# Attention and MoE on one core: a silu issued behind the next unit's copy in the first product, and the last batch's queries loaded later

## The chip, the cores and the metric

The kernel runs on one core of a Trainium2 chip. Times are device microseconds (us) of an execution. The five engines of the core that matter here are TensorE (PE, matmuls), VectorE (DVE), ScalarE (ACT), GpSimd (POOL) and SyncE (SP); POOL does no arithmetic here to speak of, it issues transfers, as SP does. All comparisons below are between runs in the fast state; one run fell into a slow state, with a lower granted clock of PE, and is named as such.

## The reference, cut to what matters

```python
# attention: batch 8, heads 8, seq 576, head_dim 64; keys and values pooled by 8
k_p = k.reshape(B, H, Sp, pool, D).mean(axis=3)
v_p = v.reshape(B, H, Sp, pool, D).mean(axis=3)
scores = scale * np.matmul(q, k_p.transpose(0, 1, 3, 2))
attn = softmax(scores)                          # cut
x = np.matmul(attn, v_p)                        # then (tokens 4608, 512)
# MoE: w_in 512 x 2048, w_out 2048 x 512
h = x @ w_in                                    # "first product"
g = h * (1.0 / (1.0 + np.exp(-h)))              # silu
out = g @ w_out                                 # "second product"
```

## The kernel before

Tokens are worked off in nine visits of 512 (t = 0 to 8). A visit has a first product (`up`), then a second one (`down_quarters`); the attention of the next batch is threaded through the second. Parts of both products are done by a scheme with seven products of quarters in place of eight. In the first product a "unit" does this for two column blocks at a time: its stages are named by digits, and `s` is a silu. `r_sb`, `rr_sb`, `t_sb` and `c_sb` are its intermediate sums, and `x_sum` are five sums of quarters of the tokens, made on DVE when a visit begins. `raw` holds keys or values before pooling, `kp` the pooled keys, `q_bf` a batch's queries and `qT` their transposes.

```python
def stage(y, n):
    if n == "2":
        product(y, 2, "P", True)                    # PE into PSUM bank P
        nc.scalar.copy(r_sb, ps["P"])               # ACT
    elif n == "5":
        product(y, 5, "Q", True)
        tt(out=rr_sb, in0=ps["Q"], in1=r_sb, op=ALU.add)      # DVE
    elif n == "1":
        product(y, 1, "R", True)
        tt(out=t_sb, in0=ps["R"], in1=rr_sb, op=ALU.subtract)
    ...
    elif n == "3":
        product(y, 3, "Q", False)                   # into Q again
        hidden(y, 0, 1, ps["Q"])                    # silu on ACT
    elif n == "7":
        product(y, 7, "P", False)
        tt(out=c_sb[0], in0=ps["P"], in1=t_sb, op=ALU.add)
        hidden(y, 0, 0, c_sb[0])                    # silu of the first sum
    elif n == "6":
        product(y, 6, "Q", False)
        tt(out=c_sb[1], in0=ps["Q"], in1=t_sb, op=ALU.add)
    else:
        hidden(y, 1, 1, c_sb[1])

# visits 2 to 8: plain blocks G, units 0 and 1
items = (G(12, 13) + [(0, "251")] + G(14) + [(0, "43")] + G(15) + [(0, "76")]
         + [(1, "2")] + [(0, "s")] + [(1, "51")] + G(0) + [(1, "43")] + G(1)
         + [(1, "76")] + G(2) + [(1, "s")] + G(3))
```

Each engine executes its own list in the order of the program. Other work (query transposes, loads, pooling) is put in as fillers at numbered steps of PE's work. The loads of the batch after next, in visits 1 to 5:

```python
def load_one(b, name):       # first half of the pooling window, plain load
    ...
    load_rows(nc.sync, raw, source(b, name)[:, :, :PH])
    ...
def load_rest(b, name):      # second half, added in flight to the first
    nc.gpsimd.dma_start(out=batches[b][f"{name}_raw"],
                        in_=source(b, name)[:, :, PH:], accum_op=ALU.add)
...
f_up.append((0, lambda: load_one(a + 1, "k")))
f_up.append((1, lambda: load_q(a + 1)))      # last batch: eight transfers of 32 x 18 x 64
f_up.append((2, lambda: load_rest(a + 1, "k")))
f_down.append((11, lambda: load_one(a + 1, "v")))
f_down.append((12, lambda: load_rest(a + 1, "v")))
...
for stage in range(2):
    f_down.append((100, lambda stage=stage: pool_k(a + 1, stage)))   # DVE reads raw
```

The stores of the output go out on SP too, sixteen a visit, ahead of the next `load_one` of k.

The softmax here doesn't subtract the row's maximum and nothing guards it: scores larger than these inputs give would overflow.

## Time and profile before

| | before |
|---|---|
| median of the first three runs | 288.31 us (288.19 to 288.97) |
| span of the profiled run | 287.0 us |
| PE busy | 279.4 us, 97% |
| length of visits 2, 3, 4, 5 | 29.4 us each |

PE is busy nearly throughout, so its busy share says little about what can be won. The useful reading is: find the steps between PE's instructions that are longer in one place than in another place with the same work. The prediction does this and shows its lines.

### The profile page before, as it was taken

How to read it: one execution, taken by the hardware profiler on the slowest of the kernel's cores; microseconds unless marked ns; L12 is line 12 of the kernel's file. 1: busy time of each engine (PE TensorE's matmuls, PEld its weight loads, DVE VectorE, ACT ScalarE, POOL GpSimd, SP SyncE). 2: the span in 40 equal slices, each digit the busy share in tenths (PEclk: the TensorE clock that was granted, in tenths of full speed). 3: DMA queues.
4: the chain of work that ended last, by engine and by line, in shares of the span. 5: the costliest groups of instructions: out<-in, count | busy, mean ns of one | idle time of the engine just before them, and what ended most of it. 6: DMA issues, size and time to landing. Idle time of an engine off the chain costs nothing.

```text
span 287.0 us, 6919 instructions
## 1 busy us (share of the span) xinstructions
PE 279.4 (97%) x2773; PEld 196.0 (68%) x2793; DVE 225.6 (79%) x403; ACT 183.4 (64%) x359; POOL 52.6 (18%) x68
## 2 busy tenths in 40 slices
PE   8989999999999999999999999999999999999995
PEld 2438544466777677767888886687667867786684
DVE  3987854979969896979797969886988786846773
ACT  1577676468656876688568857794679558325700
POOL 8754317501020011101020107212000000000000
PEclk9999999999999999999999999999999999999999
DMA  8999999893749566973979396968830032006004
GB/s 210 269 262 231 217 310 172 221 216 53 148 67 208 124 91 106 136 209 60 140 122 211 73 151 112 164 121 162 161 77 0 2 86 63 2 5 142 2 1 148
DMA packets 35296, 37.70 MB, mean 131 GB/s; under 512 B 9952, under 2 KB 27616, under 8 KB 35264
## 3 DMA queue, kind: packets, MB, share of 16 engines
q0 software_dynamic: 21760, 20.86, 43.1%
q1 hardware_dynamic: 12928, 15.48, 22.3%
q10 hardware_dynamic: 576, 0.92, 1.1%
q8 instruction: 22, 0.36, 0.6%
q14 instruction: 10, 0.08, 0.1%
HBM read 36.70 MB, written 9.44 MB: 161 GB/s over the span
## 4 chain that ended last, share of the span: by engine, by line
PE 91%; DVE 4%; ACT 2%; issue 1%; DVEq 0%
PE hp_ps L546 23%; PE o_psP L654 15%; PE o_psQ L654 15%; PE u_psQ L488 7%; PE u_psP L488 6%; PE o_psR L654 5%; PE sc_ps L351 4%; PE warm_ps L703 4%; PE o_ps L581 3%; PE nu_ps L395 3%; PE den_ps L369 2%; PE u_psR L488 2%; DVE rr_sb L508 1%; ACT r_sb L505 1%; DVE w_sum L632 1%
## 5 line engine op out<-in xcount | busy, mean ns | idle before, releaser
L546 PE MATMUL hp_ps<-xT,w_in_sb 128*128 128x512 bf16 (+3 forms) x397 | 80.8, 338 | 1.4 <-ACT h_T L552 0.4
L552 ACT ACTIVATE h_T<-hp_ps 128x512 bf16<-128x512 f32 (+2 forms) x95 | 51.3, 545 | 27.2 <-PE hp_ps L546 26.3
L654 PEld LDWEIGHTS <-h_sum 128*128 128x128 bf16 x640 | 60.6, 98 | 11.9 <-issue 1.3
L546 PEld LDWEIGHTS <-w_in_sb 128*128 128x128 bf16 x412 | 39.3, 98 | 24.9 <-issue 1.4
L614 DVE TENSOR_TENSOR h_sum<-h_T 128x1024 bf16<-128x1024 bf16 (+1 forms) x72 | 50.8, 743 | 7.0 <-ACT h_T L552 7.0
L359 ACT ACTIVATE es<-sc_ps 72x384 bf16<-72x384 f32 (+1 forms) x100 | 39.0, 470 | 10.0 <-PE sc_ps L351 10.0
L488 PEld LDWEIGHTS <-w_sum 128*128 128x128 bf16 x300 | 29.3, 98 | 8.2 <-DVE x_sum L455 0.5
L654 PEld LDWEIGHTS <-h_T 128*128 128x128 bf16 x256 | 24.1, 98 | 4.4 <-issue 0.9
L496 ACT ACTIVATE h_T<-c_sb 128x512 bf16<-128x512 f32 x30 | 18.8, 628 | 11.6 <-DVE c_sb L520 11.6
L404 DVE TENSOR_TENSOR xT<-nu_ps,rec 128x384 bf16<-128x384 f32 (+1 forms) x50 | 24.0, 533 | 0.4
L378 ACT ACTIVATE lnd<-den_ps 128x384 f32<-128x384 f32 (+1 forms) x23 | 11.1, 484 | 20.2 <-PE den_ps L369 20.2
L153 DVE STREAM_TRANSPOSE qT<-q_bf 128x576 bf16<-128x576 bf16 x32 | 23.0, 754 | 0.0
L182 POOL DMA_DIRECT2D raw<-in_k_dram x5 | 7.0, 1405 | 66.3 <-DVE qT L153 31.2
L274 DVE TENSOR_TENSOR raw<-raw 128x384 f32<-128x384 f32 (+3 forms) x20 | 12.3, 616 | 7.2 <-DMA raw<-in_v_dram 3.6
L654 PE MATMUL o_psP<-w_out_sb,h_sum 128*128 128x256 bf16 x128 | 17.6, 273 | 0.0
L654 PE MATMUL o_psQ<-w_sum,h_sum 128*128 128x256 bf16 x128 | 16.7, 273 | 0.0
L654 PE MATMUL o_psQ<-w_out_sb,h_sum 128*128 128x256 bf16 x128 | 16.6, 273 | 0.0
L654 PE MATMUL o_psP<-w_sum,h_T 128*128 128x256 bf16 x128 | 16.5, 273 | 0.0
L654 PE MATMUL o_psQ<-w_sum,h_T 128*128 128x256 bf16 x128 | 16.5, 273 | 0.0
L182 POOL DMA_DIRECT2D raw<-in_v_dram x5 | 6.9, 1390 | 49.4 <-DMA raw<-in_v_dram 15.6
L654 PE MATMUL o_psR<-w_sum,h_sum 128*128 128x256 bf16 x128 | 15.7, 273 | 0.0
L558 POOL DMA_DIRECT2D out_dram<-o_sb x1 | 0.6, 628 | 81.8 <-issue 81.8
(77 smaller groups left out, 435.9 us busy)
## 6 DMA issues: line engine op xcount, KB each, us to landing
out_dram<-o_sb SPq DMA_DIRECT2D x128, 64.0 KB, 3.0
q_bf<-in_q_dram POOLq DMA_DIRECT2D x6, 576.0 KB, 11.1
raw<-in_k_dram SPq DMA_DIRECT2D x6, 512.0 KB, 5.7
raw<-in_k_dram POOLq DMA_DIRECT2D x5, 576.0 KB, 9.6
raw<-in_v_dram POOLq DMA_DIRECT2D x5, 576.0 KB, 9.1
raw<-in_v_dram SPq DMA_DIRECT2D x5, 512.0 KB, 8.2
w_in_sb<-in_moe_w_in_dram POOLq DMA_DIRECT2D x8, 256.0 KB, 8.3
w_out_sb<-in_moe_w_out_dram POOLq DMA_DIRECT2D x4, 512.0 KB, 13.8
```

Source lines behind the costliest of these rows:

```text
L153: nc.vector.transpose(out=st["qT"][:, a, f * QF : (f + 1) * QF].rearrange("r i c p -> r (i c p)"), in_=st["q_bf"][:, a, f * n : (f + 1) * n],)
L182: nc.gpsimd.dma_start(out=batches[b][f"{name}_raw"], in_=source(b, name)[:, :, PH:], accum_op=ALU.add,)
L274: nc.vector.tensor_add(out=raw[..., :w], in0=raw[..., :w], in1=raw[..., w : 2 * w])
L351: nc.tensor.matmul(sc[s][:, cs], lhsT=kz[b % 2][rows, g, c, :], rhs=st["qT"][rows, g, i0:i1, c, :], start=(c == 0), stop=(c == 1),)
L359: nc.scalar.activation(es[:, s, :], sc[s], func=AF.Exp, scale=score_scale)
L404: nc.vector.tensor_mul(out=xT[:, 2 * g0 + c : 2 * (g0 + ng - 1) + c + 1 : 2, cols], in0=nu[c][:, :w].rearrange("r (g n) -> r g n", g=ng), ...
L488: nc.tensor.matmul(ps[bank][:, u, :], lhsT=w[:, kk, 128 * u : 128 * (u + 1)], rhs=x[:, kk, :], start=first and u == 0 and kk == 0, stop=kk ...
L496: nc.scalar.activation(h_T[:, g : g + 2, j * NQ : (j + 1) * NQ], src, func=AF.Silu)
L546: nc.tensor.matmul(hp_ps[:, r0:r1], lhsT=w_in_sb[:, kk, g * 128 : (g + 1) * 128], rhs=xT[:, kk, x0 : x0 + r1 - r0], start=(kk == 0), stop= ...
L552: nc.scalar.activation(h_T[:, g, n0 : n0 + n], hp_ps[:, :n], func=AF.Silu)
L614: nc.vector.tensor_tensor(out=h_sum[n][:, ks, :], in0=quarter(*a, ks), in1=quarter(*b, ks), op=op)
L654: nc.tensor.matmul(ps[b][:, c, :], lhsT=left(n, kt, c), rhs=W_OUT[n][:, kt, :], start=b not in begun, stop=kt == k1 - 1, skip_group_check= ...
```

## The change

Its intent is twofold. Part A: in visits 2 to 8 the silu of unit 0's first sum is issued on ACT behind unit 1's copy `r_sb` instead of ahead of it (a new stage `h`). Part B: the query load of the last batch, the one made of eight small transfers, is issued at step 48 of visit 5's first product instead of step 1, and so behind the second half of k.

```diff
-                KF if len(it) == 3 else 2 * len(it[1].strip("s")) for it in items
+                KF if len(it) == 3 else 2 * len(it[1].strip("hs")) for it in items
...
                 tt(out=c_sb[0], in0=ps["P"], in1=t_sb, op=ALU.add)
-                hidden(y, 0, 0, c_sb[0])
...
+            elif n == "h":
+                hidden(y, 0, 0, c_sb[0])
...
-                    + [(0, "76")] + G(10) + [(0, "s")] + G(11, 0, 1, 2, 3)
+                    + [(0, "7h6")] + G(10) + [(0, "s")] + G(11, 0, 1, 2, 3)
...
-                    + [(1, "2")] + [(0, "s")] + [(1, "51")] + G(0) + [(1, "43")] + G(1)
-                    + [(1, "76")] + G(2) + [(1, "s")] + G(3)
+                    + [(1, "2")] + [(0, "hs")] + [(1, "51")] + G(0) + [(1, "43")] + G(1)
+                    + [(1, "7h6")] + G(2) + [(1, "s")] + G(3)
...
-                f_up.append((1, lambda: load_q(a + 1)))
+                f_up.append((48 if a + 1 == B - 1 else 1, lambda: load_q(a + 1)))
```

## The prediction

> **What bounds the kernel now.** I read the page's busy shares first, then the chain that ended last, then the timeline of the first product ("up") of visits 2 to 8. A visit is one pass of 512 tokens, nine in all (0 to 8).
>
> ```profile
> PE 279.4 (97%) x2773; PEld 196.0 (68%) x2793; DVE 225.6 (79%) x403; ACT 183.4 (64%) x359; POOL 52.6 (18%) x68
> ...
> PE 91%; DVE 4%; ACT 2%; issue 1%; DVEq 0%
> ```
>
> TensorE (PE) carries 91% of the chain. What a scheduling change can win is only the rest: stretches in which PE waits. The chain in order of time names one such stretch in every visit from 2 to 6: the copy r_sb on ACT (0.57), then rr_sb on DVE (0.70), then PE on u_psQ. Visit 3, by the timeline (start, length, engine, line, operation; weight loads and lines of no use here left out):
>
> ```profile
> 121.03 0.65 DVE L520 TENSOR_TENSOR c_sb<-u_psP,t_sb 128x512 f32<-128x512 f32 x1
> ...
> 121.61 0.67 DVE L524 TENSOR_TENSOR c_sb<-u_psQ,t_sb 128x512 f32<-128x512 f32 x1
> 121.72 0.63 ACT L496 ACTIVATE h_T<-c_sb 128x512 bf16<-128x512 f32 x1 [1.07 <-DVE c_sb L520]
> ...
> 122.26 0.57 ACT L505 COPY r_sb<-u_psP 128x512 f32<-128x512 f32 x1
> ...
> 122.86 0.69 DVE L508 TENSOR_TENSOR rr_sb<-u_psQ,r_sb 128x512 f32<-128x512 f32 x1 [0.57 <-ACT r_sb L505]
> 122.89 0.60 PE L488 MATMUL u_psP<-x_sum,w_in_sb 128*128 128x256 bf16 x4
> ...
> 123.60 0.60 PE L488 MATMUL u_psQ<-x_sum,w_in_sb 128*128 128x256 bf16 x4
> ```
>
> Read it from the bottom. The second unit's product 3 goes into the bank u_psQ. That bank must first be read by rr_sb, rr_sb needs r_sb, and the copy to r_sb stands on ACT behind the silu of the first unit's c_sb[0]. That silu waited 1.07 us for DVE, while u_psP (started 120.72, 0.60 long) was there to be copied from 121.32. Undisturbed, one product's start follows another's by 0.44; visit 7 shows it:
>
> ```profile
> 241.46 0.60 PE L488 MATMUL u_psP<-x_sum,w_in_sb 128*128 128x256 bf16 x4
> ...
> 241.90 0.60 PE L488 MATMUL u_psQ<-x_sum,w_in_sb 128*128 128x256 bf16 x4
> ```
>
> In visit 3 the step is 0.71, so PE loses 0.27. The same subtraction gives 0.27 in visit 2 (93.52 to 94.23), 0.22 in 4 (152.31 to 152.97), 0.27 in 5, 0.29 in 6 (211.66 to 212.39), and nothing in 7 and 8. There DVE has no query transposes ahead of c_sb, so it is on time. Sum 1.32 us.
>
> A second loss stands in visit 6 alone. It comes from the loads, so I read POOL's, SP's and DVE's timelines of visits 5 and 6:
>
> ```profile
> 174.31 1.37 POOL L182 DMA_DIRECT2D raw<-in_v_dram  x1 [11.37 <-DVE kp L193]
> 175.13 5.23 POOL L138 DMA_DIRECT2D q_bf<-in_q_dram  x7
> 185.68 0.67 POOL L138 DMA_DIRECT2D q_bf<-in_q_dram  x1 [5.32 <-DMA raw<-in_v_dram]
> 192.60 1.42 POOL L182 DMA_DIRECT2D raw<-in_k_dram  x1 [6.25 <-DVE vp L193]
> ...
> 184.94 1.24 SPq L173 DMA_DIRECT2D raw<-in_k_dram  x2
> ...
> 202.21 1.22 DVE L188 TENSOR_TENSOR raw<-raw 72x1024 f32<-72x1024 f32 x1 [0.56 <-DMA raw<-in_k_dram]
> ```
>
> The last batch's queries are eight small transfers instead of one. While they are in flight, the first half of k (issued 184.94) took 6.9 us to land against 5.7 for the same transfer in visit 4, and the accumulating second half was issued 7.7 us after it, against 6.4 in visit 4 (155.16 to 161.55). So DVE waited 0.56 at the pooling of k, its five x_sum came late, and PE paid. Against visit 2, counted from the start of the visit (84.71 and 202.22, the latter with the one matmul record that is missing put back), u_psR is 0.39 late, product 3 of unit 0 is 0.60 late, and unit 1 starts 0.60 late. That 0.60 is the whole loss.
>
> **What the Trainium skill says.** "PSUM — Partial Sum Buffer", section "Engine vs sequencer instructions": ScalarE and VectorE queues are strict FIFO. The trace agrees: u_psP was ready at 121.32 and ACT idle, yet the copy started at 122.26, after the silu ahead of it. "DMA: Bandwidth & Descriptors", section "Anatomy of one DMA — SWDGE (gpsimd) path": a DMA's semaphore wait happens on the issuing sequencer. Hence a waiting transfer holds up everything behind it on POOL; the 5.32 us before the eighth query transfer agrees. Same page, section "Queues, rings and completion order": the engines take turns among queues packet by packet and take one ring's descriptors in order. So queries behind an accumulating load in POOL's queue should land after it. The v half issued at 174.31 took 11.1 us to land (185.4), the first query transfer landed at about 186.0: agreed. The same page's "Specifications" puts the smallest transfer at line rate at 512 B; the last batch's query rows are 64 floats, 256 B. The trace agrees in part: this v half took 11.1 us with those queries behind it, against 9.2 and 9.1 in visits 3 and 4 with a single big query transfer behind it.
>
> **The change part by part.** No instruction is added or removed. The edit of the string strip only alters the number of steps counted, and no filler lies between the old and the new end. In visit 1 "7h6" puts the silu where it was. What moves is this.
>
> Part A, in visits 2 to 8: on ACT, r_sb's copy comes ahead of silu(c_sb[0]). Visit 2: ACT is free at 91.28, u_psP is done at 91.95, so the copy runs from about 92.0 to 92.57 instead of from 92.89 to 93.46. rr_sb then waits for c_sb[1] ahead of it on DVE, which starts at 92.24; such operations follow each other at 0.61, so rr_sb starts at 92.85 instead of 93.49, 0.64 earlier. The bank is free 0.74 after that start (93.49 to 94.23 in the old order), at 93.59. PE wants it at 93.52 + 0.44 = 93.96. The wait of 0.27 vanishes with 0.37 to spare. The silu of c_sb[0] moves from 92.35 to about 92.5, and that of c_sb[1] from 93.36 to about 93.0, so ACT ends this stretch earlier. The other visits have the same offsets. Gain: all of 0.27 + 0.27 + 0.22 + 0.27 + 0.29 = 1.32 us, nothing in 7 and 8. PE stays saturated behind the place, so I expect no give-back.
>
> Part B, in visit 5 alone: the second k half goes ahead of the queries on POOL. Its first half lands without query traffic. By visit 4's times (k issued 11.7 into the visit, 6.4 to the second half, 10.1 to landing) it lands 28.2 into the visit. DVE wants it 28.76 into visit 4 (143.44 to 172.20), and 28.5 once that visit is 0.27 shorter. So it arrives in time with 0.3 to spare, and 0.60 comes back, if visit 4's times hold. But seven query transfers are now issued right behind it, as they were behind the v half that needed 11.1 us. If that costs 1 to 2 us again, k is late by 0.7 to 1.7 and PE loses that much where it now loses 0.60. On top, POOL has eight semaphores that go round; by the waits in the changed program the eighth query transfer now waits for the k half to land, as it waited for the v half before. It lands about 6.5 after that (185.68, 6.5 to landing). With k landing near 200.6 of the new time that is 207.2. The second transpose of visit 6 needs it at about 206.9, or 207.3 before PE feels it through DVE's slack of 0.37. That is just on the edge. A late k delays the deadline too, so the two losses do not simply add.
>
> I weigh full recovery (+0.60) at a half, a small or equal loss (about 0) at three in ten, and a loss of some 0.7 beyond the present one at two in ten: 0.30 + 0 - 0.14, about 0.2 us.
>
> Sum: 1.32 + 0.2 = 1.5 us; 288.31 - 1.5 = 286.8.
>
> **The rivals.** First: both parts work in full. Then it is 1.32 + 0.60 = 1.9 us, 286.4. For it speaks that visit 4, without small queries, shows no wait at k. Second: the late queries become the new wait, k's second half slowed by the small packets behind it or the transposes of visit 6 waiting for the eighth transfer. For it speak the 11.1 us and the edge worked out above; the time would be 287.0 to 288.0, with visit 6 the longer one. Third: part A's wait is replaced by another, silu(c_sb[0]) now late for the h_sum operations or c_sb[1] on DVE holding rr_sb. Against it: h_sum starts at 94.89 in visit 2 and needs silus that end before 94, and rr_sb has 0.37 to spare. It would leave about half of the 1.32, so 287.5. Fourth: the gap is hidden anyway and the visit is as long as before. Against it: visits 2 to 5 are each 29.36 to 29.39 long, PE is on the chain through them, and no transfer is awaited there. It would be 288.3.
>
> **Range and chances.** The sure part gives 287.0, the full one 286.4. Repeats of the kernel before spread from 288.19 to 288.97. I take 286.0 to 287.9. A gain over 2% would need 5.8 us, three times the waits in reach; a loss over 2% would need queries late by several us. Faster 0.01, within 2% 0.98, slower 0.01.
>
> **What would show it.** Part A is right if in visits 2 to 6 the copy r_sb of unit 1 starts before the silu of c_sb[0], rr_sb follows c_sb[1] without waiting for ACT, the step from u_psP to u_psQ is 0.44, and visits 2 to 5 last about 29.1. Part B is right if DVE no longer waits for raw at the end of visit 5 and unit 1 of visit 6 starts 6.6 into it. It is wrong if that wait grows, or if a transpose of visit 6 shows a wait for q_bf's transfer. The prediction as a whole fails if the five steps close and the visits keep their length, or if visit 6 grows by more than the 1.3 that part A saves.

## The result, and the profile after

The changed kernel took 287.26 us in the median of six runs (286.08 to 287.70), the kernel before 288.55 (288.19 to 289.28) in six. The ratio is 0.9947, 95% interval 0.9922 to 0.9971. Ratios here and below are the mean time of one kernel's fast runs over that of the other's fast runs of the same rounds, so they are not quite the ratio of the medians quoted. Executions over 1.5% slower than the fastest of the same kernel are left out of the means. It is about 1.5 us faster: within 2%, and inside the predicted range.

In the changed kernel the sum `c_sb[1]` is at L523 instead of L524, and the lines behind the unit's stages are one higher (L546 became L547). Its page has these two lines (busy time, and the chain's shares by engine):

```profile
PE 278.0 (98%) x2773; PEld 196.0 (69%) x2793; DVE 225.1 (79%) x403; ACT 183.8 (65%) x359; POOL 52.2 (18%) x68
...
PE 94%; DVE 3%; ACT 1%; issue 1%; DVEq 0%
```

PE's share of the chain went from 91% to 94%; DVE's fell from 4% to 3% and ACT's from 2% to 1%. Visit 3 by the timeline, to be held against the same visit in the prediction:

```profile
120.42 0.65 DVE L520 TENSOR_TENSOR c_sb<-u_psP,t_sb 128x512 f32<-128x512 f32 x1
...
120.79 0.59 ACT L505 COPY r_sb<-u_psP 128x512 f32<-128x512 f32 x1 [0.77 <-PE u_psP L488]
...
121.00 0.67 DVE L523 TENSOR_TENSOR c_sb<-u_psQ,t_sb 128x512 f32<-128x512 f32 x1
121.28 1.15 ACT L496 ACTIVATE h_T<-c_sb 128x512 bf16<-128x512 f32 x2
...
121.59 0.67 DVE L508 TENSOR_TENSOR rr_sb<-u_psQ,r_sb 128x512 f32<-128x512 f32 x1
122.27 0.60 PE L488 MATMUL u_psP<-x_sum,w_in_sb 128*128 128x256 bf16 x4
...
122.71 0.60 PE L488 MATMUL u_psQ<-x_sum,w_in_sb 128*128 128x256 bf16 x4
```

The copy now waits for PE alone, as the bracket says. Both silus run behind it as one stretch, rr_sb follows c_sb[1] on DVE with no wait for ACT, and product 3 follows product 4 by 0.44 instead of 0.71.

The loads of visit 5, first on POOL, then SP's k, then DVE at the turn to visit 6:

```profile
188.44 1.38 POOL L182 DMA_DIRECT2D raw<-in_k_dram  x1 [13.43 <-DMA raw<-in_k_dram]
189.25 5.24 POOL L138 DMA_DIRECT2D q_bf<-in_q_dram  x7
197.50 0.67 POOL L138 DMA_DIRECT2D q_bf<-in_q_dram  x1 [3.01 <-DMA raw<-in_k_dram]
```
```profile
182.20 1.17 SPq L173 DMA_DIRECT2D raw<-in_k_dram  x2
```
```profile
200.32 1.21 DVE L188 TENSOR_TENSOR raw<-raw 72x1024 f32<-72x1024 f32 x1
...
205.91 2.09 DVE L153 STREAM_TRANSPOSE qT<-q_bf 128x576 bf16<-128x576 bf16 x3
```

Neither the pooling of k nor the transposes show a wait any more. POOL stood at k's second half until 188.44, and the eighth query transfer waited for that half to land at about 197.2. It landed itself 6.3 us after its issue, at 203.8.

Where did the time go? A convenient measure is the time from unit 0's first matmul in visit 2 to the same matmul in visit 7: 86.43 to 234.51 = 148.08 us before, 86.08 to 232.33 = 146.25 after, 1.83 us less. The rest of the 2.2 us between the two spans lies ahead of visit 2 (0.35), where the change does nothing; that is run-to-run scatter.

### The profile page after: what moved, and what is told of

It reads as the page before. It is cut to its first block, busy times and chain, and to the rows that moved or that the text cites. A ratio compares the mean times of both kernels' runs of the same rounds, so it can differ in the third digit from the quotient of the medians.

```text
span 284.8 us, 6920 instructions
## 1 busy us (share of the span) xinstructions
PE 278.0 (98%) x2773; PEld 196.0 (69%) x2793; DVE 225.1 (79%) x403; ACT 183.8 (65%) x359; POOL 52.2 (18%) x68
## 4 chain that ended last, share of the span: by engine, by line
PE 94%; DVE 3%; ACT 1%; issue 1%; DVEq 0%
PE hp_ps L547 25%; PE o_psP L655 15%; PE o_psQ L655 15%; PE u_psQ L488 7%; PE u_psP L488 7%; PE o_psR L655 5%; PE sc_ps L351 4%; PE warm_ps L704 4%; PE o_ps L582 3%; PE nu_ps L395 3%; PE u_psR L488 2%; PE den_ps L369 2%; DVE w_sum L633 1%; PE kz_ps L296 1%; DVE xT L404 1%
## 5 line engine op out<-in xcount | busy, mean ns | idle before, releaser
L547 PE MATMUL hp_ps<-xT,w_in_sb 128*128 128x512 bf16 (+3 forms) x397 | 80.8, 338 | 1.4 <-ACT h_T L553 0.4
L547 PEld LDWEIGHTS <-w_in_sb 128*128 128x128 bf16 x412 | 39.3, 98 | 25.0 <-issue 1.4
L488 PEld LDWEIGHTS <-w_sum 128*128 128x128 bf16 x300 | 29.4, 98 | 7.7
L378 ACT ACTIVATE lnd<-den_ps 128x384 f32<-128x384 f32 (+1 forms) x23 | 11.1, 484 | 20.2 <-PE den_ps L369 20.2
L496 ACT ACTIVATE h_T<-c_sb 128x512 bf16<-128x512 f32 x30 | 18.1, 625 | 5.0 <-DVE c_sb L520 5.0
L274 DVE TENSOR_TENSOR raw<-raw 128x384 f32<-128x384 f32 (+3 forms) x20 | 12.4, 618 | 7.5 <-DMA raw<-in_v_dram 4.3
L520 DVE TENSOR_TENSOR c_sb<-u_psP,t_sb 128x512 f32<-128x512 f32 x15 | 10.2, 678 | 7.1 <-PE u_psP L488 3.6
L655 PE MATMUL o_psP<-w_sum,h_sum 128*128 128x256 bf16 x128 | 15.4, 272 | 0.0
## 6 DMA issues: line engine op xcount, KB each, us to landing
q_bf<-in_q_dram POOLq DMA_DIRECT2D x6, 576.0 KB, 11.1
w_out_sb<-in_moe_w_out_dram POOLq DMA_DIRECT2D x4, 512.0 KB, 13.5
```

What stands on the lines that cost most here:

```text
L274: nc.vector.tensor_add(out=raw[..., :w], in0=raw[..., :w], in1=raw[..., w : 2 * w])
L488: nc.tensor.matmul(ps[bank][:, u, :], lhsT=w[:, kk, 128 * u : 128 * (u + 1)], rhs=x[:, kk, :], start=first and u == 0 and kk == 0, stop=kk ...
L496: nc.scalar.activation(h_T[:, g : g + 2, j * NQ : (j + 1) * NQ], src, func=AF.Silu)
L547: nc.tensor.matmul(hp_ps[:, r0:r1], lhsT=w_in_sb[:, kk, g * 128 : (g + 1) * 128], rhs=xT[:, kk, x0 : x0 + r1 - r0], start=(kk == 0), stop= ...
L655: nc.tensor.matmul(ps[b][:, c, :], lhsT=left(n, kt, c), rhs=W_OUT[n][:, kt, :], start=b not in begun, stop=kt == k1 - 1, skip_group_check= ...
```

## The experiments

For every trace I read three things from the starts of the unit's products, in visits 2 to 6:

- *steps*: how much longer than 0.44 the step from unit 1's product 4 (u_psP) to product 3 (u_psQ) is, summed over the visits. Part A is to close these.
- *late*: how much later than 2.61 us after unit 0's first product its product 3 starts, summed. This is what a late k costs: DVE waits, the five x_sum come late, PE waits for them.
- *T*: the time from visit 2 to visit 7 as above.

| kernel | what it is | steps | late | T | median us | ratio to before |
|---|---|---|---|---|---|---|
| before | | 1.32 | 0.61 | 148.08 | | |
| after | A and B | 0 | 0.14 | 146.25 | 287.26 | 0.9947 |
| after_again | the same | 0 | 0.82 | 146.94 | 287.62 | 0.9945 |
| a_only | A | 0 | 1.00 | 147.11 | 287.61 | 0.9952 |
| b_only | B | slow | slow | slow | 288.74 | 0.9984 |
| b_again | B | 1.31 | 0.37 | 147.82 | 288.35 | 0.9977 |
| t_later | before, one transpose moved | 0 | 2.02 | 148.50 | 288.84 | 1.0002 |
| q_at_3 | A and B, queries at step 3 | 0 | 0.61 | 146.73 | 287.09 | 0.9937 |
| k_pool | A and B, early k | 0 | 0.01 | 146.13 | 286.59 | 0.9913 |
| k_pool_a_only | A, early k | 0 | 0.01 | 146.13 | 286.69 | 0.9908 |
| k_pool_b_only | B, early k | 1.30 | 0.01 | 147.42 | 287.77 | 0.9942 |
| q_last | A and B, queries behind v | - | - | 157.27 | 298.04 | 1.0300 |

T is 146.13 + steps + late to within 0.02 us in every row that has the three numbers, except t_later (0.35 over) and q_last. So the two losses explain this stretch of the kernel. The kernel before ran at a median of 288.55 to 289.61 beside them, with runs from 288.13 to 290.88.

All outputs are right.

**a_only: part A without part B.**

```diff
-                f_up.append((48 if a + 1 == B - 1 else 1, lambda: load_q(a + 1)))
+                f_up.append((1, lambda: load_q(a + 1)))
```

> Part A alone: the copy r_sb ahead of the first unit's silu in every visit, the last queries loaded where they were. Theory (the two waits are separate and add): the steps from u_psP to u_psQ in unit 1 of visits 2 to 6 close from 0.71 to 0.44, which is 1.3 us; the late k at the end of visit 5 stays and grows by up to 0.3 because the visit is shorter, so the whole is 1.0 to 1.3 us faster than before and visit 6 still starts its unit 1 late by 0.6 to 0.9. Rival (A's gain is eaten by the k loads, which then become the limit): less than 0.6 us faster, with DVE waiting for raw in several visits.

Measured: 0.9952 (0.9926 to 0.9977), 1.4 us faster by the means. The five steps closed. But DVE waited for k, above all at the end of two visits:

```profile
113.50 1.22 DVE L188 TENSOR_TENSOR raw<-raw 72x1024 f32<-72x1024 f32 x1 [0.57 <-DMA raw<-in_k_dram]
...
201.25 1.22 DVE L188 TENSOR_TENSOR raw<-raw 72x1024 f32<-72x1024 f32 x1 [0.18 <-DMA raw<-in_k_dram]
```

The first of these is at the end of visit 2, which the theory did not have: visit 3 lost 0.62 by it. At the turn to visit 6 the loss was 0.23, less than the 0.60 of before. The lateness of k differs from visit to visit and run to run. In the trace as a whole A's 1.32 was cut by 0.39 of extra lateness. The rival had the mechanism, though not its size in the time.

**b_only and b_again: part B without part A** (the query line of the change alone, in the kernel before).

> Part B alone: the last queries behind the second half of k, the ACT order as before. Theory: the steps of 0.71 stay in visits 2 to 6, the wait of DVE for k at the end of visit 5 is gone and unit 1 of visit 6 starts 6.6 into it instead of 7.24; 0.6 us faster than before. Rival (late queries become the new wait): a transpose of visit 6 waits for the query transfer and the time is the same as before or longer.

Measured: 0.9984 (0.9961 to 1.0007), 0.5 us by the means, but one of six runs took 357.99 us, and that was the profiled one. Its clock row on the page:

```profile
PEclk9777777777777777777777777777777777777777
```

A trace at this clock cannot be compared with the others.

> Part B alone again, as its profile fell on a run with a lowered clock (0.755). Theory as before: steps of 0.71 stay, DVE does not wait for k at the end of visit 5, unit 1 of visit 6 starts about 6.6 into it; ratio 0.997 to 0.999. Rival: visit 6 still late, ratio 1.000.

Measured: 0.9977 (0.9952 to 1.0001), 0.7 us. The steps stayed at 1.31 in sum, and unit 1 of visit 6 starts as early in the visit as in visit 2 (4.92 after unit 0's first product, 5.52 in the kernel before). The 0.60 came back. But visit 5 was 0.36 late, with DVE waiting 0.30 for the k of visit 4, which B does not touch. Taken together the two sets speak for the predicted 0.6, though each interval includes no change, and both are held against largely the same runs of the kernel before.

**t_later: the third query transpose behind the two sums on DVE, in the kernel before; ACT's order untouched.**

```diff
-            q_at = [15, 16, 17, 8] if t > 1 else [24, 25, 26, 2] if t else [82, 84, 86, 88]
+            q_at = [15, 16, 40, 8] if t > 1 else [24, 25, 26, 2] if t else [82, 84, 86, 88]
```

> The kernel before with one line changed: the third query transpose of visits 2 to 6 stands behind the first unit's two sums on DVE instead of ahead of them; the ACT order is as before. If the 0.27 comes about because c_sb[0] is late on DVE and the copy stands behind its silu, then c_sb[0] is 0.7 earlier, the silu and the copy move with it, and the step closes to 0.44 as in visits 7 and 8: 1.0 to 1.3 us faster than before. Rival (the step is lost to the bank or to rr_sb itself, and the ACT order is what matters whatever DVE does): the step stays above 0.6 and the time is as before.

Measured: 1.0002 (0.9974 to 1.0030). A miss on the time, a hit on the mechanism. All five steps closed to 0.44 with the silu still ahead of the copy; visit 3:

```profile
122.58 0.60 PE L488 MATMUL u_psP<-x_sum,w_in_sb 128*128 128x256 bf16 x4
...
123.02 0.60 PE L488 MATMUL u_psQ<-x_sum,w_in_sb 128*128 128x256 bf16 x4
```

So the 0.27 comes from c_sb[0] being late on DVE *and* the copy standing behind its silu; taking away either ends it. The gain was then given back, in this trace by k, at the end of visit 2 (0.47) and above all of visit 5:

```profile
202.23 1.22 DVE L188 TENSOR_TENSOR raw<-raw 72x1024 f32<-72x1024 f32 x1 [1.44 <-DMA raw<-in_k_dram]
```

The table's *late* is 2.02 here. The further 0.35 of T lies in the second product and comes from the edit itself: the moved transpose now stands ahead of unit 1's sums. Against k_pool, in visit 2, unit 1's c_sb[0] starts 9.91 after unit 0's first product instead of 9.53, the fourth `es` on ACT at 15.15 instead of 14.81, and the four `den_ps` matmuls that read `es` take 0.43 instead of 0.35. PE loses 0.05 to 0.10 there in each of the five visits.

**k_pool: the changed kernel with k's first half issued on POOL, so that it does not stand behind SP's stores.**

```diff
-        load_rows(nc.sync, raw, source(b, name)[:, :, :PH])
+        load_rows(nc.gpsimd if name == "k" else nc.sync, raw, source(b, name)[:, :, :PH])
```

> The changed kernel with the first half of k issued on POOL instead of SP, where it stood behind sixteen stores of the visit before. In the changed kernel's trace k landed at 142.0 and 171.2 just when DVE wanted it, and DVE was 0.1 late in visits 4 and 5; its six runs spread over 1.6 us. Theory (late k in some runs makes the spread and holds back part of A's gain): k lands some 8 us earlier, the time is 0.3 to 0.8 us below the changed kernel's and the runs agree within 0.8. Rival (the spread is from elsewhere, such as the first visits' loads): the time and the spread are those of the changed kernel, ratio to the kernel before 0.995.

Measured: 0.9913 (0.9892 to 0.9935), 2.5 us faster than before, six runs within 0.93 us (0.8 was expected). In the same visit 5:

```profile
172.88 1.34 POOL L173 DMA_DIRECT2D raw<-in_k_dram  x2 [3.97 <-DVE kp L193]
179.94 1.42 POOL L182 DMA_DIRECT2D raw<-in_k_dram  x1 [5.72 <-DMA raw<-in_k_dram]
```

The first half waits only for the pooling that frees its buffer, the second half follows at 179.94 instead of 188.44, and the lateness is gone from every visit.

**after_again: the changed kernel once more.**

> The changed kernel once more, unaltered, for a second trace beside the next three on one chip. Theory (the time of a run is set by how late k lands in visits 2 to 4, which differs from run to run): ratio to the kernel before 0.993 to 0.996, runs spread over 1 us or more, and in this trace at least one visit from 3 to 6 starts its product 3 of unit 0 late (over 2.61 after its first product), or DVE waits for raw. Rival: every visit is as regular as in visit 2 and the spread lies ahead of visit 2.

Measured: 0.9945 (0.9908 to 0.9981), six runs from 286.74 to 288.67. This time it was visit 4 that paid:

```profile
142.06 1.22 DVE L188 TENSOR_TENSOR raw<-raw 72x1024 f32<-72x1024 f32 x1 [0.80 <-DMA raw<-in_k_dram]
...
145.07 0.61 PE L488 MATMUL u_psR<-x_sum,w_sum 128*128 128x256 bf16 x4 [0.46 <-DVE x_sum L455]
```

These two lines are the ends of the path: DVE waits 0.80 for k, x_sum is late, PE waits for x_sum. Product 3 of that visit started 3.43 after the first product instead of 2.61, so 0.82 was lost. In the first trace of the same kernel the loss was 0.14. T is therefore 0.69 longer here, and yet the two profiled runs took 286.74 and 286.69: in this one visit 2 began at 85.35, in the first at 86.08. So the rival holds too. Ahead of visit 2 the fast traces scatter by as much (85.35 to 86.43), and which share of the spread between runs is late k is not shown. The runs of k_pool, which has none of it, still spread over 0.93.

**k_pool_b_only: early k, part B, ACT's order of before** (the k line of k_pool in b_only).

> Early k (first half on POOL) and part B, with the ACT order of the kernel before. With late k out of the way this against the run with early k and both parts (0.9913) is part A alone. Theory: the steps of unit 1 are 0.71 again in visits 2 to 6, k is in time, and the ratio is 0.9913 + 1.32 / 289 = 0.996. Rival (part A is worth less than its five gaps because something behind them gives it back): ratio 0.993 or lower.

Measured: 0.9942 (0.9913 to 0.9972); expected was 0.996. Held against k_pool_a_only of the same rounds (it lacks part B, which the next run finds to be worth nothing with early k), part A is worth 287.77 - 286.69 = 1.1 us by the medians, and 147.42 - 146.13 = 1.29 in the traces. The steps were back with 1.30. The trace confirms A's size. The ratio alone would not separate 1.3 from 1.0.

**k_pool_a_only: early k, part A, queries where they were before** (the k line of k_pool in a_only).

> Early k and part A, with the last queries where they were in the kernel before, ahead of k's second half. With early k, k's second half of visit 5 is issued after the eighth query transfer, some 13 into the visit, and lands some 23 into it, where DVE wants it at 28.5. Theory (part B is worth something only because k is late): same as early k with both parts, ratio 0.990 to 0.993. Rival (the small query transfers cost time in themselves, by what they do to the other transfers): slower than that by 0.5 us or more, ratio over 0.993.

Measured: 0.9908 (0.9879 to 0.9937), the same as k_pool, and T is the same to the hundredth. With k early, the place of the queries is worth nothing. Part B therefore gained by moving k forward on POOL and by letting it land sooner, not by sparing PE or DVE anything else.

**q_last: the queries one place further back, behind the second half of v.**

```diff
-                f_up.append((48 if a + 1 == B - 1 else 1, lambda: load_q(a + 1)))
+                (f_down if a + 1 == B - 1 else f_up).append((13 if a + 1 == B - 1 else 1, lambda: load_q(a + 1)))
```

> The changed kernel with the last queries behind the second half of v, one place further back on POOL. In the changed kernel the eighth query transfer landed at 203.8 and the second transpose of visit 6 wanted it at about 206.6. Behind v, which is issued near 198, the first seven land near 207 to 210 and the eighth, which then waits for v to land near 207, at about 213. Theory (the place of the queries has 3 us of room and no more): a transpose of visit 6 waits for them, and the time is 5 to 7 us longer than the changed kernel's. Rival (there is more room than that, the transposes' delay is hidden): within 1 us of the changed kernel.

Measured: 1.0300 (1.0257 to 1.0343), 10.4 us over the changed kernel of the same rounds. On DVE and PE:

```profile
214.03 0.78 DVE L153 STREAM_TRANSPOSE qT<-q_bf 128x576 bf16<-128x576 bf16 x1 [8.60 <-DMA q_bf<-in_q_dram]
...
218.45 1.01 PE L488 MATMUL u_psQ<-x_sum,w_in_sb 128*128 128x256 bf16 x4 [8.64 <-DVE rr_sb L508]
```

The first transpose waited for its queries, and PE stood for 8.64 us behind rr_sb. The direction was right, the size too small: the transfers came later than estimated, and PE came back slow. The windows of this stretch (busy us and counts of PE, PEld, DVE, ACT and POOL, then PE's granted clock):

```profile
208.00:210.00 2.00, 1.76 (x12) 1.09 (x12) 0.00 (x0) 0.32 (x1) 0.32 (x1) 1.00 1.96 183
...
214.00:216.00 2.00, 0.00 (x0) 0.00 (x0) 1.59 (x3) 0.00 (x0) 0.00 (x0) 0.50 0.07 8
...
220.00:222.00 2.00, 2.00 (x8) 1.03 (x7) 0.40 (x1) 0.70 (x2) 0.00 (x0) 0.50 0.00 0
```

At 220, with PE working again, its clock is still half.

**q_at_3: the queries at step 3 instead of 48, still behind k's second half.**

```diff
-                f_up.append((48 if a + 1 == B - 1 else 1, lambda: load_q(a + 1)))
+                f_up.append((3 if a + 1 == B - 1 else 1, lambda: load_q(a + 1)))
```

> The changed kernel with the last queries at step 3 of the first product instead of step 48, which is still behind k's second half on POOL. Theory (what counts is the order on POOL, since POOL stands at k's second half until its first half has landed, far past step 48): the same POOL timeline and the same time as the changed kernel, ratio to before 0.993 to 0.997. Rival (the step counts, because the queries are then in flight earlier): the first query transfer is issued before 180 and the time is that of part A alone or worse.

Measured: 0.9937 (0.9914 to 0.9960), the changed kernel's time. POOL's timeline is the changed kernel's:

```profile
189.09 1.38 POOL L182 DMA_DIRECT2D raw<-in_k_dram  x1 [14.02 <-DMA raw<-in_k_dram]
189.90 5.23 POOL L138 DMA_DIRECT2D q_bf<-in_q_dram  x7
```

POOL is held at k's second half from 175.07, when v's second half has been issued, until k's first half has landed. The number 48 has no effect; only the order on POOL has.

## Why the prediction was right or wrong

The time was right: 286.8 predicted, 287.26 measured; a gain of 1.5 us was worked out, and it was 1.3 us by the medians and 1.5 by the ratio. That the sum fits so well is partly luck: part B was counted at 0.2 and gave about 0.6, and late k, which took some of it back, was not counted. The two errors have opposite signs. By its steps:

- **Part A's 1.32 us: right.** All five steps closed in every fast trace with A (but for visit 6 of q_last, where PE stood for the queries), and visits 2 to 5 took 29.10 to 29.23 in the changed kernel's first trace instead of 29.4. The early-k pair puts A at 1.29 in the trace. The counter-test t_later shows that the cause was the one named, the silu's late input with the copy behind it.
- **"PE stays saturated behind the place, so I expect no give-back": wrong.** So was the remark under the fourth rival that no transfer is awaited in visits 2 to 5. In the kernel before, k landed 2.6 us ahead of its use in visit 2, 1.1 in visit 3 and 0.6 in visit 4 (issue of the second half plus its time to landing, against the start of the pooling). A shortened visit takes 0.27 off that, and the landing scatters by more: even in visit 2 k was late in a_only and t_later, where its first half went out 12.2 and 12.4 into the visit instead of 9.8. The traces with part A and late k lost 0.14, 0.82, 1.00 and 0.61 in all; those with early k lost 0.01. Late k is the term that the sum did not have. In the first trace of the changed kernel it was small, in others not. How much of it part A causes is not shown: the kernel before was traced once (0.61), and b_again, without part A, lost 0.37.
- **Part B's recovery: right in mechanism, sized too low.** Unit 1 of visit 6 starts in time in all four traces of kernels with B behind k (after, after_again, b_again, q_at_3). I gave full recovery a half and counted 0.2; it was full each time, 0.60 against the one trace of the kernel before. Other traces without B lost 0.24 (a_only) and 1.49 (t_later) at this place. The mis-sized terms were two. First, k was expected to be issued 11.7 into the visit and was issued 10.4 into it: 182.20 less the visit's start at 171.81, which is 1.72 ahead of its first unit product. In the other traces of that order it was 10.5 to 10.7, against 12.1, 12.4 and 13.8 where the queries are early (before, t_later, a_only). The prediction had taken 11.7 from visit 4 as a visit without query traffic. But visit 4 has its own query load in flight, one transfer issued 1.8 into the visit and landed at 14.9, and visit 5 of the changed kernel has none until k has gone out. Second, k's second half was expected to take 10.1 to land, or more with small transfers behind it, and took 8.8. In the four traces of that order it took 8.5 to 8.8 with seven small transfers right behind it, so the reading that these slowed the half ahead of them (v's 11.1) is not borne out. k landed at 197.2, and the eighth query transfer at 203.8 instead of 207.2. What was called "just on the edge" had 2.8 us to spare before the second transpose, which starts about 0.7 after 205.91. (The prediction's "near 200.6" for k's landing under "Part B" is 0.3 more than its own terms give: 172.84 for the start of visit 5, less 0.76 for three shortened visits, plus 28.2.)
- **The eighth transfer's wait: right.** It waited for k's half to land, 3.01 us, and landed 6.3 us after issue against the 6.5 assumed.
- **The rivals.** The late queries were a true danger, one place further back on POOL than the change put them (q_last). The first rival, both parts in full, gave 286.4; the fastest of the six runs was 286.08, and the median missed it. The third and the fourth did not come about: the steps closed and the visits became shorter. Late k in part of the runs is a cause that the traces show; that it accounts for the whole of the median's 0.9 is not shown.

Why the first half of k goes out sooner when the queries are late is only partly shown. It stands behind SP's sixteen stores, and their issue took 12.96 us in visit 5 of the kernel before and 11.79 in the changed one; their median time to landing fell from 4.5 to 2.8. Query transfers are in flight in that time in the one and not in the other. That they are small is not needed for it: in visits 3 and 4, where the queries of a batch are one transfer, k's first half went out 10.6 to 13.3 into the visit in all eight fast traces that issue it on SP, against 10.3 to 10.7 in visit 5 where the queries come behind k. No run took the query traffic away and left all else, so the cause stays an inference.

The version that beats both is early k with part A, with or without part B: ratios 0.9908 and 0.9913. The intervals overlap those of the changed kernel, so the traces carry this verdict more than the times do: 146.13 against 146.25 and 146.94.

## What to carry to other kernels

When a closed gap shortens every turn of a loop, look at each transfer that lands within the scatter of its use: it can become the next wait, and its slack can be read before the change. One trace shows the slack but not the scatter; that takes several. In a list executed in order, what counts is which instruction stands ahead of which; the step number at which a transfer was written down was worth nothing, its neighbour on the queue everything. And where runs of one kernel scatter by as much as the gain, sum the gaps in the traces: they told apart two parts of 1.3 and 0.6 us, where the times were too scattered to do so.

## What the Trainium skill lacked or had wrong

- "DMA: Bandwidth & Descriptors", section "Anatomy of one DMA — SWDGE (gpsimd) path", fits a transfer as 2.0 us plus its bytes over 436 GB/s. For k's accumulating second half (72 x 8 x 256 floats, 590 KB) that is an estimate of 3.4 us. It took 9.8 us in visit 2 and 8.8 in visit 5 of the changed kernel's first trace, beside other traffic. The queries' load of the same size, which converts to bf16 and does not accumulate, took 13.5 in visit 3 and 11.5 in visit 4 of that trace, so a load need not accumulate to be that slow. The page has no figure for an accumulating load.
- No page gives a figure for what loads on POOL's queue do to stores on SP's. In visit 5, k behind the sixteen stores went out 12.1 to 13.8 us into the visit with the eight query transfers in flight, and 10.3 to 10.7 without; in visits 3 and 4, with one query transfer, 10.6 to 13.3.
- "TensorE: Matmul & The Clock Gate", section "What's actually happening", has PE's clock fall to half after an idle window of about 3.4 us and return after about as long a busy one. The queries' wait in q_last agrees roughly: PE was idle from 209.8 to 218.45, and the granted clock was 0.50 from about 212.5, 2.7 us into the idle time, to about 222.7, 4.3 us after PE went on. What the page does not have is the slow run of b_only: a mean granted clock of 0.755 through a whole run of one core, 357.99 us against 288.00 to 289.20 in the five others.
